# New landing places for the last raw weight pieces, and first products ahead of second sums in a chunked RWKV7 kernel

## The chip, the cores and the metric

The kernel runs on one core of a Trainium2 chip. The metric is the device time of one execution in microseconds (us), of which medians are quoted. Before the change it was 901.05 us (median of 3 runs, 900.12 to 902.5). All times inside an execution come from a profile of one execution and count from its first instruction. In the profile PE is TensorE, PEld its weight loads, DVE VectorE, ACT ScalarE, POOL GpSimd, and SPq the queue from which SyncE issues transfers. In the lines shown, `ph` is a PSUM bank of a first product, `gts` its Silu, `po` a bank of a sum (or of a merge), `wo_s` the converted w_out, `room` a landing place, `XI` and `mi` the inverse and its tile; `[2.06 <-DVE XI L426]` says that the engine was idle for 2.06 us until VectorE had written `XI` in line 426.

## The reference

```python
# r,k,v,w,a,b: (4 batches, 8 heads, 768 steps, 40 channels), float32
for t in range(S):
    y[:, :, t] = einsum('bhd,bhde->bhe', rt, state)
    Sa = einsum('bhde,bhe->bhd', state, at)
    state = state * wt[..., None] - einsum('bhd,bhe->bhde', Sa, bt) \
          + einsum('bhd,bhe->bhde', vt, kt)
x = y.transpose(0, 2, 1, 3).reshape(3072, 320)
h = x @ w_in                                  # 320 x 2048
return (h * (1 / (1 + exp(-h)))) @ w_out      # 2048 x 320
```

The weights `w_in` and `w_out` arrive as 64-bit floats and are turned into 32-bit floats on the chip.

## The kernel before

The recurrence is worked in 12 chunks of 64 steps. Each chunk pair needs the inverse of small triangular blocks: VectorE computes it row by row, stores it (`xd`), reads it back in another layout (`XT`), transposes it, and TensorE merges the blocks. After a merge come keys, right side, solve, readings, and the state products (`pgy`). When two chunks are done, their 256 or 512 columns of x go through the token stage: "first products" x @ w_in with a Silu by ScalarE, and "second sums" with w_out. All of TensorE's work runs in one order that a scheduler fixes at build time.

The raw weights come in 40 pieces. Each lands in a place, and is converted by five VectorE and three ScalarE operations.

```python
if n < NW // 2:           place = ("wi0", "wi1", "wo0", "wo1", "room")[n % 5]
elif n < NW * 3 // 4:     place = ("wo0", "wo1", "room")[(n - NW // 2) % 3]
else:                     place = ("mi", "tmp", "room")[(n - NW // 2) % 3]   # mi, tmp: the inverse's tiles
...
def weights(n, ...):                        # conversion: first part of piece n, second part of piece n - 1
    vector.tensor_scalar(e <- hi); vector.tensor_scalar(f <- hi)
    scalar.activation(e); scalar.activation(f); scalar.activation(lo)
    ...
    vector.scalar_tensor_tensor(e); vector.tensor_tensor(f <- f + lo); vector.tensor_tensor(weight <- f * e)
    load_weights(n)                         # the place is free: send for the next piece
...
def row(t):                                 # one row of the inverse
    vector.tensor_tensor(tmp <- X * M);  vector.tensor_reduce(X <- tmp)
def back():                                 # after the last row
    scalar.copy(mi[0:16] <- X);  vector.tensor_copy(mi[16:32] <- X);  send(sync, xd, mi)
...
ph = [moe_bank("ph") for _ in range(2)]     # first product: two of three banks, free again after its Silus
...
now = {2: 4, 3: 5}[n]                       # items of the token stage done beside chunks 2 and 3
```

## Time and profile before

| | before |
|---|---|
| median time | 901.05 us |
| span of the profiled execution | 899.2 us |
| TensorE / VectorE / ScalarE / GpSimd busy | 87% / 62% / 33% / 17% |
| mean granted TensorE clock | 0.946 (its record begins at 94.7 us) |

Busy shares say little here: TensorE looks full on average, but between 205 and 270 us it waits, runs at half clock (0.50 granted from 215 to 220 us) and waits again. The prediction shows the slices, stretches and orders of time from which this is read.

### The profile page before, as it was taken

The numbers are of one execution on the slowest core, as the hardware profiler recorded it, in microseconds if no ns is written. First come the engines' busy times: TensorE is split into PE (matmuls) and PEld (weight loads), VectorE is DVE, ScalarE is ACT, GpSimd is POOL, SyncE is SP. The second block draws the span as 40 slices with busy tenths as digits, with TensorE's granted clock in tenths as the row PEclk, the third lists the DMA queues.
The fourth block names the chain that finished last, engine by engine and source line by source line (L and its number), as shares of the span: only waits on it lengthen the run. The fifth ranks groups of instructions, "written<-read, shape, count | busy, mean of one in ns | idle before, by whom it ended". The sixth has DMA issues, their size and how long they took to land.

```text
span 899.2 us, 25358 instructions
## 1 busy us (share of the span) xinstructions
PE 778.9 (87%) x10914; PEld 552.9 (61%) x10914; DVE 557.9 (62%) x1084; ACT 297.4 (33%) x689; POOL 151.4 (17%) x156
## 2 busy tenths in 40 slices
PE   2145689896898997999998999999999989999995
PEld 2135677674786853875746857648757468574643
DVE  9979889885439598176896295982768912510000
ACT  2234358532622322514025342226140243311120
POOL 7312024200202201303102240113031000000001
PEclk9999869996759998999999999999999999999998
DMA  7875646744325542444613627325424021102001
GB/s 154 167 147 142 150 130 150 166 106 107 90 59 128 105 110 47 115 108 87 145 34 62 157 64 158 93 48 117 96 56 122 16 61 40 42 23 57 1 1 33
DMA packets 240151, 82.99 MB, mean 92 GB/s; under 512 B 207136, under 2 KB 231968, under 8 KB 240032
## 3 DMA queue, kind: packets, MB, share of 16 engines
q1 hardware_dynamic: 219488, 69.96, 34.8%
q10 hardware_dynamic: 20544, 11.34, 4.7%
q8 instruction: 87, 1.43, 0.7%
q14 instruction: 32, 0.26, 0.1%
HBM read 67.11 MB, written 14.16 MB: 90 GB/s over the span
## 4 chain that ended last, share of the span: by engine, by line
PE 45%; DVE 19%; DMA 3%; SPq 2%; issue 1%; ACT 1%; POOL 0%; POOLq 0%; ACTq 0%; DVEq 0%
PE po L825 14%; PE ph L813 9%; DVE tmp L419 7%; DVE XI L426 7%; PE pgy L264 4%; PE pl L264 3%; PE ph L818 3%; PE pm L264 2%; SPq L217 2%; PE pt L264 2%; PE pr L264 2%; PE po L264 2%; PE pq L264 2%; PE pu L264 2%; DVE GV L761 1%
## 5 line engine op out<-in xcount | busy, mean ns | idle before, releaser
L825 PE MATMUL po<-wo_s,gts 128*128 128x320 f32 x768 | 224.8, 448 | 17.1 <-ACT gts L820 10.8
L825 PEld LDWEIGHTS po<-wo_s,gts 128*128 128x128 f32 x768 | 145.2, 194 | 82.7 <-ACT gts L820 14.7
L813 PE MATMUL ph<-xt,wi_s 128*128 128x512 f32 (+1 forms) x448 | 182.2, 549 | 2.2 <-ACT ot L834 1.4
L813 PEld LDWEIGHTS ph<-xt,wi_s 128*128 128x128 f32 x448 | 82.1, 192 | 82.3 <-issue 67.9
L820 ACT ACTIVATE gts<-ph 128x512 f32<-128x512 f32 (+1 forms) x112 | 54.6, 531 | 161.1 <-PE ph L818 160.4
L722 DVE TENSOR_TENSOR vl<-pl,ml 128x512 f32<-128x512 f32 x48 | 30.9, 685 | 113.0 <-PE pl L264 77.6
L419 DVE TENSOR_TENSOR tmp<-XI,mi 64x2 f32<-64x2 f32 (+40 forms) x169 | 85.5, 506 | 8.8 <-DMA mi<-md 3.9
L841 POOL TENSOR_TENSOR ot<-gts,ot 128x320 f32<-128x320 f32 x24 | 21.8, 907 | 358.1 <-ACT gts L839 352.9
L336 DVE RECIPROCAL w<-W 128x512 f32<-128x512 f32 x24 | 80.3, 3347 | 1.3
L426 DVE TENSOR_REDUCE XI<-tmp 64x2 f32<-64x2 f32 (+40 forms) x169 | 77.0, 455 | 5.2
L264 PE MATMUL pq<-XT,sb 32*32 32x32 f32 (+1 forms) x1280 | 34.9, 207 | 32.6 <-DVE XT L463 21.1
L818 PE MATMUL ph<-xt,wl_s 64*128 64x512 f32 (+1 forms) x224 | 56.9, 585 | 0.0
L264 PE MATMUL pm<-a,kb 64*64 64x64 f32 x1280 | 41.5, 244 | 16.9 <-POOL kb L366 15.5
L264 PEld LDWEIGHTS pq<-XT,sb 32*32 32x32 f32 (+1 forms) x1280 | 31.6, 131 | 38.7 <-issue 16.0
L363 POOL TENSOR_TENSOR a<-a,W 64x512 f32<-64x512 f32 x32 | 39.5, 1236 | 75.4 <-DMA a<-in_aT 52.2
L1084 DVE TENSOR_SCALAR bad<-pb 1x1 int32<-1x1 f32 x1 | 0.1, 147 | 83.4 <-PE pb L1083 83.4
L264 PEld LDWEIGHTS pm<-a,kb 64*64 64x64 f32 x1280 | 38.1, 156 | 21.2 <-POOL kb L366 15.7
L839 ACT COPY gts<-po 128x320 f32<-128x320 f32 x24 | 10.2, 425 | 121.8 <-PE po L825 98.0
L264 PEld LDWEIGHTS pl<-r,vut 64*128 64x128 f32 x768 | 45.4, 189 | 4.7 <-ACT vl L650 2.1
L264 PE MATMUL pl<-r,vut 64*128 64x64 f32 x768 | 46.5, 274 | 2.0 <-ACT vl L650 2.0
L264 PE MATMUL pt<-ident,kb 128*128 128x128 f32 x192 | 29.1, 313 | 21.2 <-DVE a L308 21.2
L348 POOL TENSOR_TENSOR kb<-kb,w 128x512 f32<-128x512 f32 x20 | 24.8, 1238 | 131.9 <-DVE w L336 118.6
(108 smaller groups left out, 1060.7 us busy)
## 6 DMA issues: line engine op xcount, KB each, us to landing
kb<-in_bT SPq DMA_DIRECT2D x48, 128.0 KB
vut<-in_vT SPq DMA_DIRECT2D x48, 128.0 KB
r<-in_rT SPq DMA_DIRECT2D x24, 256.0 KB
w<-in_wT SPq DMA_DIRECT2D x45, 128.0 KB
kb<-in_kT SPq DMA_DIRECT2D x44, 128.0 KB
a<-in_aT SPq DMA_DIRECT2D x32, 128.0 KB
vl<-in_v SPq DMA_DIRECT2D x48, 80.0 KB
xs<-yx ACTq DMA_DIRECT2D x48, 80.0 KB
```

The lines of the kernel that those rows point to most:

```text
L264: x = what(*x, **y)
L336: pin(nc.vector.reciprocal(R, u.W[:, :, 1 : C + 1]))
L348: nc.gpsimd.tensor_tensor(out=u.kb[:, :, 1], in0=u.kb[:, :, 1], in1=R, op=ALU.mult)
L363: nc.gpsimd.tensor_tensor(out=u.a[J, j], in0=u.a[J, j], in1=u.W[J, :, 0:C], op=ALU.mult)
L419: x = nc.vector.tensor_tensor(out=part, in0=X[L, :, t + 1 : N, t + 1 : N], in1=M[L, :, t, t + 1 : N].unsqueeze(2).to_broadcast([hi - lo, I ...
L426: x = nc.vector.tensor_reduce(out=X[L, :, t + 1 : N, t], in_=part, axis=AX.X, op=ALU.add)
L722: nc.vector.tensor_tensor(out=u.vl[:, :, j, D:], in0=pl[j].rearrange("p (q t) -> p q t", q=Q), in1=ml.unsqueeze(1).to_broadcast([128, Q, C ...
L813: in_order(nc.tensor.matmul(ph[n], lhsT=wi_s[:, k, at : at + 128], rhs=xt[:, k, :], start=k == 0, stop=False))
L818: in_order(nc.tensor.matmul(ph[n], lhsT=wl_s[R, i, :], rhs=xt[R, 2, :], start=False, stop=True))
L820: nc.scalar.activation(out=place(2 * i + n)[:, T], in_=ph[n], func=AF.Silu)
L825: in_order(nc.tensor.matmul(po[:, 0:DM], lhsT=place(f)[:, b * 128 : b * 128 + 128], rhs=wo_s[:, NF // 2 * half + f, :], start=f == 0, stop ...
L841: nc.gpsimd.tensor_tensor(out=ot4, in0=rest, in1=ot4, op=ALU.add)
```

## The change

The intent: the last pieces land where nothing of the inverse waits for them (the k and b tiles of later chunks, and a stretch of w_out), and TensorE has eight first products to do before the first sum that needs the last weights.

```diff
-            elif n < NW * 3 // 4:
+            elif n < NW // 2 + 9:
                 place = ("wo0", "wo1", "room")[(n - NW // 2) % 3]
+            elif n == NW // 2 + 12:
+                place = "wo1"
             else:
-                place = ("mi", "tmp", "room")[(n - NW // 2) % 3]
+                place = ("room", "kb2", "kb3")[(n - NW // 2 - (8 if n < NW // 2 + 12 else 9)) % 3]
...
-            u.kb = sb.tile([128, Q, 2, C], F32, name="kb", bufs=6)
+            u.kb = sb.tile([128, Q, 2, C], F32, name="kb", tag=f"kb{(NM * u.n + u.m) % 6}")
...
         for half in range(2):
+            sums = []
             for c in range(2 if apart else 1):
                 steps += [partial(first, T, NF // 4 * half + i) for i in range(NF // 4)]
-                steps += [partial(second, half, b) for b in range(T.start // 128, T.stop // 128)]
+                sums += [partial(second, half, b) for b in range(T.start // 128, T.stop // 128)]
+                if half == 0 or c > 0 or not apart:
+                    steps += sums
+                    sums = []
...
-        for u in units[n + 2]:
+        for u in units[n + 2] if n == 3 else []:
             load(u)
-        now = {2: 4, 3: 5}[n]
+        now = {2: 6, 3: 4}[n]
-            weave(steps[0:4], queue[0:1], [x[i] for i in (0, 5, 1, 6)], convert[31:34])
+            weave(steps[0:4], queue[0:1], convert[31:])
...
-            convert[34:] if n == 2 else [],
```

After the change, a line of the kernel has a number 4 higher than before from the conversions on: the second sum is L829 and not L825, the Silu L824, the first product L817.

More of the change, by code (lines that the diff above doesn't have):

```diff
@@ L980 @@
         steps = [x for pair in zip(*[chain(u, xs) for u in units[n]]) for x in pair]
-        now = {2: 4, 3: 5}[n]
+        now = {2: 6, 3: 4}[n]
         x = prepare(n + 2)
         if n == 2:
-            weave(steps[0:4], queue[0:1], [x[i] for i in (0, 5, 1, 6)], convert[31:34])
-            scores = [x[i] for i in (2, 4, 7, 9, 3, 8)]
+            weave(steps[0:4], queue[0:1], convert[31:])
+            scores = [partial(load, u) for u in units[n + 2]] + [x[i] for i in (0, 5, 1, 6, 2, 4, 7, 9, 3, 8)]
         else:
```

## The prediction

> **What bounds the kernel now.** I read four views in this order. First the page's slices, for where TensorE has room: a slice is 899.2 / 40 = 22.5 us.
>
> ```profile
> PE   2145689896898997999998999999999989999995
> ...
> PEclk9999869996759998999999999999999999999998
> ```
>
> From slice 13 on (about 290 us) TensorE is busy at 9 or 10 tenths, except near 350 us, so late work is bounded by TensorE. Before that stand slices 9 to 11 (202 to 270 us): 6, 8 and 9 tenths, at a granted clock of 0.6, 0.7 and 0.5. That is where w_out's second half is converted from raw 64-bit words and where the inverse of chunks 2 and 3 is merged. Second, busy time in stretches there (TensorE, its weight loads, VectorE, ScalarE, GpSimd, then granted clock, DMA share, GB/s):
>
> ```profile
> 200.00:205.00 5.00, 5.00 (x24) 3.09 (x23) 4.90 (x14) 2.22 (x7) 0.00 (x0) 1.00 0.12 43
> 205.00:210.00 5.00, 2.89 (x14) 1.65 (x12) 2.19 (x7) 3.03 (x8) 0.00 (x0) 1.00 0.68 221
> 210.00:215.00 5.00, 1.41 (x2) 0.50 (x2) 1.54 (x6) 1.41 (x5) 0.00 (x0) 0.58 0.81 169
> 215.00:220.00 5.00, 3.25 (x106) 2.17 (x109) 4.21 (x8) 0.00 (x0) 0.00 (x0) 0.50 0.38 81
> ...
> 245.00:250.00 5.00, 2.83 (x38) 1.57 (x40) 2.58 (x7) 0.19 (x1) 0.80 (x2) 0.50 0.62 135
> ```
>
> At 205 us TensorE falls from full to a quarter busy and VectorE with it: both wait. Third, TensorE in order of time (start, length, line, operation, count, idle time before and its releaser); fourth, the same of VectorE and of SyncE, which issues the loads:
>
> ```profile
> 210.78 1.41 PE L825 MATMUL po<-wo_s,gts 128*128 128x320 f32 x2 [2.03 <-ACT gts L820]
> 215.88 1.44 PE L825 MATMUL po<-wo_s,gts 128*128 128x320 f32 x2 [3.68 <-DVE wo_s L190]
> ...
> 247.17 2.50 PE L825 MATMUL po<-wo_s,gts 128*128 128x320 f32 x4 [2.58 <-DVE wo_s L190]
> ```
>
> ```profile
> 208.60 0.29 DVE L178 TENSOR_SCALAR room<-room 128x256 int32<-128x256 int32 x1 [2.41 <-DMA room<-in_w_out]
> 213.73 0.30 DVE L178 TENSOR_SCALAR room<-room 128x256 int32<-128x256 int32 x1 [3.05 <-DMA room<-in_w_out]
> 215.74 3.63 DVE L463 STREAM_TRANSPOSE XT<-XT 32x512 f32<-32x512 f32 x5
> ...
> 235.38 0.29 DVE L178 TENSOR_SCALAR room<-room 128x256 int32<-128x256 int32 x1 [3.27 <-DMA room<-in_w_out]
> ```
>
> ```profile
> 215.88 18.08 SPq L217 DMA_DIRECT2D room<-in_w_out  x3
> ```
>
> The second sums (L825) stand in TensorE's order before the merges and wait for w_out; w_out waits for a conversion, that for its raw piece, and that for a place: three pieces take 18 us to be issued, because their places are the inverse's own tiles and the merge's scratch. While TensorE idles its clock halves, and the merges run slowly.
>
> [...]after 2.03 + 3.68 us of gaps the granted clock is 0.50, and two matmuls of L825 take 1.44 us where sixteen take 4.57 us later (0.57 for two). [...]a conversion that waits for its data holds what is behind it, as the 3.05 us before the transposes show. [...]xd to transposes is 206.68 to 215.74 us, write, reads and issue together.
>
> **The change part by part.**
>
> *Places.* In the new order of VectorE all 40 pieces are converted before the inverse's last row; before, 33 were by then, counting the one right after it, 35 at the first transpose, and the last at 270 us. Ahead of the first row stand 35 conversions and not 31; among the rows 5 and not 2. Removed: 3.68 + 2.58 us of waits for w_out, and in the second merge the 4 us (243.1 to 247.15) in which its scratch operation stood behind three conversions. Added: 7 to 8 conversions ahead of the transposes. One is five VectorE operations starting some 0.2 to 0.34 us apart (208.60 to 210.68 us with a wait of 0.37), so 1.5 us: 8 x 1.5 = 12 us. VectorE's idle time from 110 to 205 us is 10.4 us by the stretches (1.3, 2.8, 0.6, 2.0, 1.7, 2.0), much of it waits for raw pieces that three free places shorten. If all is filled the transposes come 1.6 us later, if half 7. I take 4: they start at 220 and not at 215.7.
>
> *Order of products.* A first product of 256 columns is 8 + 4 matmuls, 1.99 + 0.63 = 2.62 us. In the new order four more of them (10.5 us) follow the four that end at 208.75 us, so TensorE has work until 219.3 us in place of 2.03 + 3.68 us of waits. But the first of the merge's products was put behind the seventh of eight: TensorE stops at 197.2 + 7 x 2.62 = 215.5 us until a transpose is there, at about 220.7. [...]The eighth and two quarters of a sum then run cold, and the bulk of the merge's first products, at 218.7 before, starts at some 227.
>
> *What is won after it.* From there to the state products (pgy, 268.85 us before) is 50.2 us now. Warm, with sums of which none waits, I count 39.5 us: first merge 10.5 (its 32-row products take 1.26 us at full clock in later chunks, 3.2 to 3.4 here), kt, right side and solve 8.2, second merge 12 (now 19.2), masks and readings 6.9 (now 8.4), plus slack. So pgy starts at about 227 + 39.5 = 266.5: won 2.3 us. From pgy to the merge of chunks 4 and 5 (357 us) VectorE's chain binds, scores to loads to 39 us of rows, and should only move along.
>
> *One item more.* Ten items of the token stage instead of nine are done in chunks 2 and 3, so one of 4.5 us leaves the TensorE-bound part. The room for it is there: at 350 to 355 us TensorE idles 3.68 + 2.04 us. Against it: the sums that covered the load of the next x (issued 322.65, products from 326.76 us) are gone, 10 us of idle at a low clock; in each later pair 17.1 us of cover becomes 12.6, which ends about when x lands (issue ends 448.2 us, first product 454.26). I take 1.3 us for these. Sum: 2.3 + 4.5 - 1.3 = 5.5 us.
>
> *Side effect.* With a tag for each k and b tile the scheduler puts ten loads of chunks 2 and 3, 128 KB each, into the first 27 us, three ahead of the first score stores. DMA is free there (82, 52 and 65 GB/s at 15 to 30 us), but the first row waited just 0.30 us for its tile, so up to 1.5 us may be lost; later load queues get shorter. Net zero.
>
> Predicted: 901.05 - 5.5, near 895.5 us.
>
> **The rivals.** *The clock is saved whole.* If VectorE fills its idle time and the transposes come at 217 us, [...]the clock stays up, the merge's bulk starts at 221 and pgy at 260.5: 8 + 3 = 11 us, or 890. For it: the scheduler put the merge's products just there, so its model has the tile ready. Against: its model before likewise showed no 3.05 us load waits. *The conversions become the bound.* The second load of the inverse's tile stands behind four loads of pieces on SyncE's queue, two of which wait for conversions; and the xd store stands behind k, b, w and a of chunks 4 and 5, which wait for the last pieces. If this costs 9 us the transposes come at 225, pgy at 272, and the item moved ahead only pays for it: 901 to 902. For it: VectorE is busy 39.4 of 40 us at 130 to 170. *The later order eats it.* If the exposed x loads cost 2 us in each of the four pairs, 899. Against: they fall where TensorE awaits the merge anyway.
>
> **Range and chances.** The transposes' arrival moves the result from 890 to 902, most likely 893 to 898; the start adds 1.5 us either way. Eight times in ten 887 to 902. Faster by over 2% means under 883 us: it needs all 13 us of idle time at 205 to 255 us and the cold part, and no delay: 0.05. Slower by over 2%, over 919 us, needs a stall of which the order shows no sign: 0.02. Within 2%: 0.93.
>
> **What would show it.** In TensorE's order of time no L825 waits for wo_s any more; its next gap is the merge's pq behind the seventh or eighth first product, waiting for the transpose of XT. In VectorE's, no conversion after the transposes, and the first transpose at 217 to 224 us. In the stretches, 205 to 220 us near full, a dip of the clock near 220, and none at 245 to 265. The state products of chunk 2 start some 2 us earlier, and the first 512-column product follows a gap. Rows beginning after 197 us, a transpose after 225 us or first scores stored later than 23 us would make the prediction too low; a clock that never falls there would make it too high.

## More of the kernel before

One more view of before is needed later, ScalarE in order of time (start, length, line, operation, count, idle time before it and what ended that):

```profile
205.58 1.07 ACT L435 COPY mi<-XI 128x512 f32<-128x512 f32 x1 [2.06 <-DVE XI L426]
206.56 0.65 ACT L820 ACTIVATE gts<-ph 128x256 f32<-128x256 f32 x2
```

ScalarE idles 2.06 us for the inverse's last row, copies, and only then does two Silus (L820).

## The result, and the profile after

The changed kernel took 909.17 us (median of 4 runs, 906.98 to 910.25) against 900.75 us of before on the same chip. The ratio is 1.0087, with a 95% interval from 1.0063 to 1.0111. A ratio is the mean time of one kernel's fast runs over that of the other's in the same rounds, so it isn't quite the ratio of the medians. A later repetition gave 1.0040. "Within 2%" held, but the time left the range, on the slow side.

The slices of the page of the changed kernel (905.1 us, so 22.6 us each):

```profile
PE   2135689998889659999998999999999989999996
...
PEclk9655868998769789999999999999999999999999
```

Counted from 0, slices 9 to 12 read 8, 8, 8, 9, so no slice there is full, and a new dip, 6 and 5, stands in slices 13 and 14 (294 to 339 us); it holds the 7.82 us for which TensorE waits for the next x, up to 339.55 us. The clock row misleads: in slices 1 to 3 it fell from 9, 9, 9 to 6, 5, 5, from 20 to 90 us by the stretches from 1.00 to 0.59. That makes up the fall of the mean from 0.946 to 0.914 (0.41 x 70 us = 29 us, and 0.032 x 905 us = 29 us). But the trace of before has no record of the clock ahead of 94.7 us, where that of the changed kernel begins at 25.2 us, and a time without a record counts as full clock: before reads 1.00 from 20 to 90 us. The products were as slow in both. Before, changed, and the same product later in the changed kernel, warm:

```profile
79.42 3.27 PE L264 MATMUL pq<-XT,sb 32*32 32x32 f32 x61 [8.17 <-DVE XT L514]
...
79.95 3.27 PE L268 MATMUL pq<-XT,sb 32*32 32x32 f32 x61 [8.32 <-DVE XT L518]
...
370.62 1.17 PE L268 MATMUL pq<-XT,sb 32*32 32x32 f32 x62 [0.38 <-DVE XT L467]
```

So the fall of the mean is no effect of the change; in the other executions of before the mean lies between 0.899 and 0.949. The sums at 188.5 us start within 0.1 us of before.

Busy time in stretches of the changed kernel (columns as in the prediction):

```profile
205.00:210.00 5.00, 4.68 (x22) 3.12 (x23) 4.90 (x10) 1.20 (x4) 2.79 (x2) 1.00 0.67 167
210.00:215.00 5.00, 1.86 (x7) 1.25 (x6) 2.91 (x5) 1.61 (x3) 0.00 (x0) 0.79 0.55 162
215.00:220.00 5.00, 5.00 (x15) 3.11 (x13) 1.62 (x3) 0.66 (x2) 0.00 (x0) 0.52 0.57 122
```

The stall moved from 205-210 to 210-215 us. It is followed by 5 us of full work at half clock. TensorE in order of time names the wait:

```profile
205.32 1.13 PE L817 MATMUL ph<-xt,wi_s 128*128 128x256 f32 x4 [1.28 <-ACT gts L824]
...
213.85 2.08 PE L817 MATMUL ph<-xt,wi_s 128*128 128x256 f32 x4 [3.14 <-ACT gts L824]
...
217.01 3.34 PE L817 MATMUL ph<-xt,wi_s 128*128 128x256 f32 x8
...
227.32 1.34 PE L829 MATMUL po<-wo_s,gts 128*128 128x320 f32 x4
...
239.76 2.50 PE L829 MATMUL po<-wo_s,gts 128*128 128x320 f32 x4
```

No sum waits for w_out any more. But a first product waits 3.14 us for a Silu (`gts`, L824), and the eight matmuls at 217.01 us take 3.34 us where eight warm ones take 1.99. Why is the Silu late? ScalarE:

```profile
212.45 1.07 ACT L439 COPY mi<-XI 128x512 f32<-128x512 f32 x1 [4.67 <-DVE XI L430]
213.42 0.65 ACT L824 ACTIVATE gts<-ph 128x256 f32<-128x256 f32 x2
```

It is the pair of lines that was shown of before, 6.9 us later. The products of these Silus were done at 209.6 us, but in ScalarE's order the inverse's copy is ahead of them and waits for the last row. And the last row is late; VectorE and then GpSimd in order of time:

```profile
196.45 0.42 DVE L194 TENSOR_TENSOR wo_s<-room 128x256 f32<-128x256 f32 x1
...
196.88 0.28 DVE L182 TENSOR_SCALAR room<-room 128x256 int32<-128x256 int32 x1
...
201.21 1.21 DVE L194 TENSOR_TENSOR wo_s<-room 128x256 f32<-128x256 f32 x1
...
202.93 1.14 DVE L182 TENSOR_SCALAR room<-room 128x256 int32<-128x256 int32 x1
...
206.53 1.41 DVE L194 TENSOR_TENSOR wo_s<-room 128x256 f32<-128x256 f32 x1
...
208.34 1.01 DVE L423 TENSOR_TENSOR tmp<-XI,mi 128x338 f32<-128x338 f32 x1
...
218.31 3.63 DVE L467 STREAM_TRANSPOSE XT<-XT 32x512 f32<-32x512 f32 x5 [5.27 <-DMA XT<-xd]
```

```profile
200.71 1.43 POOL L352 TENSOR_TENSOR kb<-kb,w 128x512 f32<-128x512 f32 x1 [52.85 <-ACT room L185]
202.74 1.18 POOL L344 TENSOR_TENSOR kb<-kb,w 128x512 f32<-128x512 f32 x1 [0.60 <-DMA kb<-in_kT]
206.19 1.47 POOL L352 TENSOR_TENSOR kb<-kb,w 128x512 f32<-128x512 f32 x1 [2.27 <-DMA kb<-in_kT]
207.62 1.36 POOL L344 TENSOR_TENSOR kb<-kb,w 128x512 f32<-128x512 f32 x1
```

Two things stand among the rows: conversions (L182, L194 and others), and operations that take two to four times as long as elsewhere (the first two lines; L423 of this size took 0.51 us before) while GpSimd multiplies k and b of chunk 4. Each of the four long ones ends within 0.4 us of the end of a GpSimd operation. In the kernel before GpSimd does nothing from 190 to 206 us.

Where the 5.9 us between the two profiled executions (905.1 - 899.2) come from, by milestones:

| milestone | before | after | difference |
|---|---|---|---|
| first of the half's first products | 197.2 | 197.3 | +0.1 |
| the last row has ended, copy starts | 205.6 | 212.4 | +6.9 |
| first transpose | 215.7 | 218.3 | +2.6 |
| bulk of the first merge's products | 218.7 | 228.6 | +9.9 |
| state products of chunk 2 | 268.9 | 279.0 | +10.1 |
| state products of chunk 3 | 306.8 | 321.1 | +14.4 |
| keys of chunk 4 | 358.9 | 371.7 | +12.9 |
| last state products | 799.3 | 812.2 | +12.9 |
| end of the last sum | 888.8 | 898.0 | +9.2 |
| end | 899.2 | 905.1 | +5.9 |

The medians differ by 8.4 us, and in the repetition by 5.2; single executions differ by a few us.

### The profile page after: what moved, and what is told of

Read it like the earlier page. It is cut to its first block, busy times and chain, and to the rows that moved or that the text cites.

```text
span 905.1 us, 25356 instructions
## 1 busy us (share of the span) xinstructions
PE 781.6 (86%) x10914; PEld 550.2 (61%) x10914; DVE 557.5 (62%) x1084; ACT 296.4 (33%) x689; POOL 150.6 (17%) x156
## 4 chain that ended last, share of the span: by engine, by line
PE 55%; DVE 33%; DMA 4%; issue 3%; ACT 3%; SPq 1%; POOL 1%; ACTq 0%; POOLq 0%; DVEq 0%
PE po L829 15%; PE ph L817 11%; DVE tmp L423 8%; DVE XI L430 8%; PE pgy L268 5%; PE pl L268 4%; PE ph L822 3%; PE po L268 3%; PE pt L268 3%; PE pq L268 3%; PE pu L268 2%; DVE w L340 2%; PE pr L268 2%; PE pm L268 2%; DVE GV L765 1%
## 5 line engine op out<-in xcount | busy, mean ns | idle before, releaser
L829 PE MATMUL po<-wo_s,gts 128*128 128x320 f32 x768 | 227.7, 452 | 10.7 <-ACT gts L824 9.3
L817 PE MATMUL ph<-xt,wi_s 128*128 128x512 f32 (+1 forms) x448 | 186.5, 559 | 15.0 <-DMA xt<-xs 8.7
L829 PEld LDWEIGHTS po<-wo_s,gts 128*128 128x128 f32 x768 | 146.8, 196 | 76.7 <-ACT gts L824 11.9
L817 PEld LDWEIGHTS ph<-xt,wi_s 128*128 128x128 f32 x448 | 83.6, 197 | 97.3 <-issue 69.4
L824 ACT ACTIVATE gts<-ph 128x512 f32<-128x512 f32 (+1 forms) x112 | 54.5, 532 | 196.4 <-PE ph L822 194.8
L423 DVE TENSOR_TENSOR tmp<-XI,mi 64x2 f32<-64x2 f32 (+40 forms) x169 | 84.5, 500 | 9.8 <-DMA mi<-md 5.1
L430 DVE TENSOR_REDUCE XI<-tmp 64x2 f32<-64x2 f32 (+40 forms) x169 | 76.7, 454 | 4.8
L845 POOL TENSOR_TENSOR ot<-gts,ot 128x320 f32<-128x320 f32 x24 | 20.9, 872 | 325.7 <-ACT gts L843 322.2
L268 PE MATMUL pm<-a,kb 64*64 64x64 f32 x1280 | 39.2, 235 | 17.5 <-POOL kb L370 15.5
L268 PE MATMUL pq<-XT,sb 32*32 32x32 f32 (+1 forms) x1280 | 30.1, 202 | 25.7 <-DVE XT L467 14.5
L843 ACT COPY gts<-po 128x320 f32<-128x320 f32 x24 | 10.2, 425 | 125.9 <-PE po L829 114.0
L268 PEld LDWEIGHTS pm<-a,kb 64*64 64x64 f32 x1280 | 36.0, 148 | 22.7 <-POOL kb L370 15.7
L268 PEld LDWEIGHTS pq<-XT,sb 32*32 32x32 f32 (+1 forms) x1280 | 27.3, 124 | 32.4 <-issue 16.0
L268 PE MATMUL pt<-ident,kb 128*128 128x128 f32 x192 | 26.9, 298 | 22.8 <-DVE a L312 22.8
L312 DVE TENSOR_TENSOR a<-pm,ml 64x512 f32<-64x512 f32 x48 | 33.0, 687 | 18.8 <-PE pm L268 18.0
```

Source lines behind the costliest of these rows:

```text
L268: x = what(*x, **y)
L312: x = nc.vector.tensor_tensor(out=u.a[O, j], in0=pm[O].rearrange("p (q t) -> p q t", q=Q), in1=ml[O].unsqueeze(1).to_broadcast([C, Q, C]), ...
L423: x = nc.vector.tensor_tensor(out=part, in0=X[L, :, t + 1 : N, t + 1 : N], in1=M[L, :, t, t + 1 : N].unsqueeze(2).to_broadcast([hi - lo, I ...
L430: x = nc.vector.tensor_reduce(out=X[L, :, t + 1 : N, t], in_=part, axis=AX.X, op=ALU.add)
L817: in_order(nc.tensor.matmul(ph[n], lhsT=wi_s[:, k, at : at + 128], rhs=xt[:, k, :], start=k == 0, stop=False))
L824: nc.scalar.activation(out=place(2 * i + n)[:, T], in_=ph[n], func=AF.Silu)
```

## The experiments

The start of the half's first products differs by up to 3.6 us between executions (196.7 to 200.3 us), whatever the kernel, so milestones of the experiments count from it. The theory after the comparison had two parts: conversions among the rows delay the inverse and, through ScalarE's queue, the Silus; and quarter sums stand between the merge's steps. Rivals: the order of products itself, the earlier loads, the throttle alone. All runs were correct; one run of before, in the third group, was slow and is left out. The first four kernels shared a chip and its runs of the kernel before; so did the next four, the next three and the last two. The wait for "gts" is the longest that TensorE spends on a Silu of the half's first products.

**order_only**: before, with the loop of the second half and `now` of the change, nothing else.

```diff
-                steps += [partial(second, half, b) ...]
+                sums += [partial(second, half, b) ...]     # as in the change
-        now = {2: 4, 3: 5}[n]
+        now = {2: 6, 3: 4}[n]
```

> The kernel before with the order of the products alone (eight first products ahead of the four sums, ten items of the token stage in place of nine); places, tags and loads stay as before. Theory (the loss of 8.4 us has two parts: conversions among the inverse's rows hold ScalarE's copy and with it the Silus, about 8 us by the start of the merge; quarter sums between the merge's products, about 2 us more than they cost before; and the item moved ahead gives 4.5 us back): here only two conversions stand among the rows, so they end near 206 us, no gap of 3 us waits for gts, the merge's first products run near 219 us, but the sums still stand between the merge's steps: 896 to 903 us. Rival (the order itself is the loss, whatever the places): 905 to 910 us.

Measured: 903.26 us against 903.27, ratio 0.9986 (0.996 to 1.0012). The rows ended 8.6 us after the first product (before 8.4), the longest wait for gts in this stage was 0.86 us. The rival falls: the order by itself costs nothing, and gains nothing either. State products of chunk 2 came 77.1 us after the first product (before 71.6), which the item moved ahead would about pay back.

**places_only**: the changed kernel with the old order of products.

```diff
-        now = {2: 6, 3: 4}[n]
+        now = {2: 4, 3: 5}[n]          # and steps += [second ...] directly after each four firsts
```

> The changed kernel with the old order of the products (four firsts, two sums, four firsts, two sums; nine items); places, tags and loads as changed. Theory: the conversions among the rows stay, so the rows end near 212 us and ScalarE's copy still stands ahead of Silus, but TensorE has sums to do there that need no Silu of a late product: the gap for gts is shorter, yet the transposes come at 218 us and not 215.7, so pgy of chunk 2 starts 2 to 6 us later than 268.85, and no item is moved ahead: 902 to 909 us. Rival (only the order costs): at or below the time before, 895 to 901 us.

Measured: 915.06 us, ratio 1.0132 (1.0103 to 1.016). That is worse than expected: the rows ended 15.7 us after the first product. The loss belongs to the places.

**act_free**: the changed kernel, ScalarE's half of the copy given to VectorE.

```diff
-            nc.scalar.copy(out=mi[L, 0:16], in_=turned[L, 0:16])
+            if N == 16 and hi - lo == 128:
+                nc.vector.tensor_copy(out=mi[L, 0:16], in_=turned[L, 0:16])
+            else:
+                nc.scalar.copy(out=mi[L, 0:16], in_=turned[L, 0:16])
```

> The changed kernel, with ScalarE's half of the inverse's last copy (chunks 2 and 3 only) given to VectorE. Theory (Silus queued behind that copy on ScalarE stop TensorE for 3.14 us, and the clock falls after it): the gap before the first product at 213.85 us shrinks below 1 us, the clock stays at 0.9 or more from 205 to 220 us, the first products end near 221 us in place of 227.3, and the kernel is 4 to 7 us faster than the changed one: 902 to 905 us. The copy costs VectorE 0.6 us ahead of the transposes. Rival (the first products run late for another cause, such as the throttle alone): the gap goes, the clock falls nevertheless, 907 to 910 us.

Measured: 906.55 us, ratio 1.0033 (0.9994 to 1.0072). The stretches of this run:

```profile
210.00:215.00 5.00, 5.00 (x26) 3.45 (x24) 3.81 (x7) 1.32 (x4) 0.00 (x0) 1.00 0.55 155
215.00:220.00 5.00, 2.54 (x14) 1.88 (x14) 1.26 (x2) 0.66 (x2) 0.00 (x0) 0.94 0.59 150
```

The gap is gone and the clock stays up, so the copy in ScalarE's queue was the cause of the stall. The first products ended at 225.6 us, not near the 221 that was expected. The state products of chunk 2 came 76.2 us after the first product, not 81.7. In time the interval overlaps that of the unaltered kernel, so what this stall costs at the end isn't separated from zero. TensorE now stops later, for the transpose.

**sums_late**: the changed kernel, the four sums of the second half behind the merge of chunk 3.

```diff
+                    mark["merged"] = product(...).ins          # in the merge's last product
...
+                if n0 == 0 and half == 1 and f == 0:
+                    behind(x, mark["merged"])                   # order on TensorE only
```

> The changed kernel with the four second sums of chunks 0 and 1 (second half) held behind the last product of the merge of chunk 3; nothing else moved by hand. Theory (the quarter sums between the merge's steps stand on the path): the time from the merge's first products to pgy of chunk 2 falls from 50.3 us to 40 to 44 us, the sums go into the idle time before the 512-column products (7.82 us wait for xt and the rows' chain), and the kernel is 4 to 9 us faster than the changed one: 900 to 905 us. Rival (the sums fill time in which the merge waits for VectorE and ScalarE anyway, and keep the clock up): the merges take as long without them, the clock there is lower, and the time stays 907 to 912 us.

Measured: 899.84 us, ratio 0.9973 (0.9947 to 0.9999): faster than the changed kernel. But from the merge's bulk to the state products it took 46.9 us, not 40 to 44; 3.1 us more were won between the state products of chunks 2 and 3 (39.0 in place of 42.2). TensorE in the first merge of this run:

```profile
228.84 0.25 PE L268 MATMUL po<-XT,qq 32*16 32x16 f32 x8 [0.62 <-DVE qq L488]
...
230.74 0.22 PE L268 MATMUL po<-XT,qq 32*16 32x16 f32 x3 [1.19 <-issue]
...
234.47 0.23 PE L268 MATMUL po<-qq,XT 32*32 32x16 f32 x1 [1.82 <-issue]
...
235.58 3.27 PE L268 MATMUL pq<-XT,sb 32*32 32x32 f32 x61 [0.51 <-DVE XT L518]
```

Even without a sum, one step, the completion of the corners, lasts from 228.84 to about 235 us, and the clock falls (0.6 in the page's slices from 224 to 269 us): the 61 products after it take 3.27 us, where 62 of this form take 1.17 to 1.19 us when warm.

**conv_late**: the changed kernel, conversions of the last three pieces behind the last row.

```diff
+            after_rows = lambda x: behind(x, mark["row"])
+            convert[37:] = [partial(weights, i, after_rows) for i in range(37, NW + 1)]
             weave(steps[0:4], queue[0:1], convert[31:])
```

> The changed kernel with the conversions of the last three pieces (37, 38, 39) held behind the inverse's last row, so that they run while the inverse's tile is stored and read back; the sums stay between the merge's steps. Theory (the changed places lose because conversions stand among the rows: the rows ended at 212.4 us and not 205.6, the Silus waited behind ScalarE's copy): rows end near 208 us, transposes at 213 to 215 us, no gap of 3 us for gts, and the kernel is 4 to 8 us faster than the changed one: ratio to before 0.999 to 1.005. Rival (the places lose by their tags and the earlier loads, or the sums are all of it): rows end earlier but the time stays within 2 us of the changed kernel, ratio 1.007 to 1.010.

Measured: 897.28 us against 904.11, ratio 0.9922 (0.9898 to 0.9946), more than was expected. The stretches and VectorE's order:

```profile
205.00:210.00 5.00, 5.00 (x24) 3.21 (x23) 4.79 (x11) 1.80 (x5) 0.00 (x0) 1.00 0.00 0
210.00:215.00 5.00, 4.15 (x21) 2.72 (x20) 4.11 (x14) 3.77 (x12) 0.00 (x0) 1.00 0.65 194
215.00:220.00 5.00, 5.00 (x28) 3.36 (x24) 4.37 (x8) 1.32 (x4) 0.00 (x0) 1.00 0.75 127
```

```profile
208.97 0.60 DVE L440 COPY mi<-XI 128x512 f32<-128x512 f32 x1
...
216.00 3.63 DVE L467 STREAM_TRANSPOSE XT<-XT 32x512 f32<-32x512 f32 x5
```

The conversions fill the 7 us in which the inverse is stored and read back, when VectorE idled 5.27 us in the changed kernel. Rows ended 8.9 us after the first product, the longest wait for gts was 1.13 us, the clock never fell from 205 to 220 us, and state products of chunk 2 came after 72.1 us. More than the conversions moved here: GpSimd's products of chunk 4 and the loads for them came after the rows too (pool_late, below), and what each of them is worth in time isn't separated.

**conv_sums**: both repairs.

> Both repairs: the last three conversions behind the rows, and the four second sums behind the merge of chunk 3. Theory (two separate losses that add: sums_late won 11 us against the changed kernel's ratio, act_free 5 us by the same stall that this one removes): 4 to 8 us below sums_late: ratio to before 0.989 to 0.993. Rival (the two repairs win the same idle time): the ratio of sums_late, 0.996 to 0.999.

Measured: 894.68 us, ratio 0.9894 (0.987 to 0.9919): the version that beats both kernels, 1.1% under before. The further gain over conv_late is 2.6 us by the medians, less than the sums were worth alone; the intervals just overlap.

**order_sums**: order_only with the sums behind the merge, as in sums_late.

> The kernel before with the order of the products (as in order_only) and the sums behind the merge of chunk 3; places, tags and loads as before. Theory (the new places are worth nothing by themselves, the order wins once the sums are out of the merge): order_only stood at 0.9986, so 4 to 9 us less: ratio 0.989 to 0.995. Rival (without the new places the sums or the merge's scratch wait for conversions: the scratch operation of the second merge stood behind three conversions up to 247 us): ratio 0.997 or above.

Measured: 901.39 us, ratio 0.9963 (0.9933 to 0.9992). It fell between theory and rival. The new places are therefore worth something once the conversions are off the rows (conv_sums, with the same sums: 0.9894).

**tags_only**: before, with a tag of its own for each k and b tile.

```diff
-            u.kb = sb.tile(..., name="kb", bufs=6)
+            u.kb = sb.tile(..., name="kb", tag=f"kb{(NM * u.n + u.m) % 6}")
```

> The kernel before with a tag of its own for each k and b tile, nothing else: ten loads of chunks 2 and 3 go out in the first 27 us. Theory (the hoisted loads cost nothing, as the traces agree up to 197 us): ratio 0.998 to 1.002. Rival (part of the loss of the changed places, 11.8 us in places_only, is from the hoisted loads or from what the tags do later): 1.004 or above.

Measured: 901.9 us against 904.11, ratio 0.9983 (0.9951 to 1.0015). The rival falls: the tags cost nothing.

**after_again**: the changed kernel unaltered, beside the two that follow.

> The changed kernel unaltered, beside the repaired ones on the same chip. Ratio to before 1.006 to 1.011 as on the first chip (1.0087); if the chip or the day mattered, the ratio would fall outside.

Measured: 906.12 us against 900.88, ratio 1.0040 (1.0002 to 1.0078), below the expected span. Its rows ended 15.1 us after the first product and the wait for gts was 3.14 us, both as the first time. The size of the loss is known to be between 0 and 1% and no better; its sign and its place are.

**conv_one**: as conv_late, for the last piece alone (`convert[39:]`).

> A dose: only the conversion of the last piece (39) is held behind the inverse's last row, not of the last three. Theory (each conversion among the rows delays the rows by some 1.5 us, and the stall for gts goes as the copy moves ahead): rows end about 13 us after the first of the half's first products started (8.9 with three held, 15.1 with none), the gap for gts is 1 to 2.5 us, ratio to before 1.001 to 1.006, between the changed kernel (1.0087) and three held (0.9922). Rival (what helps is something else than the number of conversions, such as the order of SyncE's queue): ratio equal to one of the two ends.

Measured: 908.87 us, ratio 1.0068 (1.0027 to 1.0109). Rows ended after 12.1 us, as expected, but the gap for gts was 1.97 us and the clock still fell, to 0.60 from 212 to 215 us. Less than the whole repair gave no gain in time: the rows moved as the theory had it, but the ratio lies with the unaltered kernel's, as the rival had it. In this run two of GpSimd's products were among the rows, in conv_late none.

**conv_pgy**: as conv_sums, but the sums wait for the state products of chunk 2.

```diff
+                mark["written", (be + j) % 2] = product(...).ins   # in the state products
...
+                    behind(x, mark["written", 0]); behind(x, mark["written", 1])
```

> As conv_sums, but the four sums wait for the last state product of chunk 2 and not for the merge of chunk 3, so that no sum stands between the state products of its second pair. Theory (the sum in the middle of the state products delays VectorE's chain to the next state): pgy of chunk 3 follows that of chunk 2 within 38 us (39.9 in conv_sums), ratio to before 0.986 to 0.989. Rival (the products of masks there, not the sum, set the time): ratio as conv_sums, 0.989 to 0.991.

Measured: 895.02 us, ratio 0.9922 (0.9885 to 0.9958), no better than conv_sums. State products of chunk 3 followed after 42.4 us and not 39.9. TensorE there:

```profile
295.73 1.13 PE L268 MATMUL pm<-stage,kb 64*64 64x64 f32 x32 [8.82 <-POOL kb L352]
...
299.47 1.13 PE L268 MATMUL pm<-stage,kb 64*64 64x64 f32 x32 [2.61 <-POOL kb L352]
```

The theory falls. Without sums there TensorE just waits 8.82 us for GpSimd, and the products that follow run cold (1.13 us where 0.69 is warm).

**pool_late**: the changed kernel, GpSimd's four products of chunk 4 behind the last row. conv_late had moved both conversions and these products; this run moves the products alone.

```diff
             x = nc.gpsimd.tensor_tensor(out=u.kb[:, :, 1], in0=u.kb[:, :, 1], in1=R, op=ALU.mult)
+            if u.n == 4:
+                behind(x, mark["row"], Sync)        # likewise for kb[:, :, 0]
```

> The changed kernel, with the four GpSimd products of k and b with the reciprocals of chunk 4 held behind the inverse's last row; conversions and sums as changed. In the changed kernel these four run at 200 to 209 us, among the rows, and four VectorE operations beside them took 1.21, 1.14, 1.41 and 1.01 us where their like take 0.42, 0.29, 0.42 and 0.51: 3.1 us together; in the kernel before, and with the last three conversions held, no GpSimd work falls there. Theory (of the 6.7 us by which the rows end later, some 3 are this contention, and the rest the three more conversions): no VectorE operation among the rows takes over 0.7 us, the rows end some 12 us after the half's first product (15.1 in the changed kernel, 8.9 with three conversions held), the gap for gts shrinks from 3.14 to 1 to 2 us, ratio to before 1.000 to 1.007. Rival (the lengthened operations are idle time that would pass anyway, all 6.7 us are the conversions): rows end 15 us after, ratio 1.004 to 1.010.

Measured: 904.47 us against 904.22, ratio 0.9997 (0.9955 to 1.0039). The rows ended 11.9 us after the first product, no operation among them took over 0.7 us, and the wait for gts was 1.42 us, with the clock at 1.00 from 205 to 215 us. So 3.2 of the 6.7 us of the rows' delay were contention between VectorE and GpSimd (the four lengthened operations had lost 3.1 us), and the other 3.5, by difference, the conversions. In time the interval overlaps that of the unaltered kernel. The transposes did not come earlier (20.9 us after the first product, 21.0 in the changed kernel). SyncE's queue shows what took up most of the gain:

```profile
209.67 0.34 SPq L221 DMA_DIRECT2D xd<-mi  x1
212.52 1.89 SPq L221 DMA_DIRECT2D w<-in_wT  x3
214.50 4.29 SPq L221 DMA_DIRECT2D XT<-xd  x8
```

From the store of the inverse to its reading back it was 2.64 us in the changed kernel (213.54 to 216.18 us), here 4.83: three loads of w stand ahead, and the queue waited 2.4 us for one of the moved products (`kb`, L344). The moved products held up SyncE's queue.

**pool_sums**: pool_late and sums_late together.

> As pool_late, with the four sums behind the merge of chunk 3 as well. Theory (the repairs add): 2 to 4 us below sums_late (0.9973), ratio 0.992 to 0.996, and above conv_sums (0.9894), in which the conversions left the rows too. Rival: as sums_late, 0.996 to 0.999.

Measured: 895.36 us, ratio 0.9926 (0.9884 to 0.9968). That is what repairs that add would give, but the interval overlaps that of sums_late (0.9947 to 0.9999), so that they add isn't shown.

| kernel | last row after first product, us | longest wait for gts in the half's first products, us | state products of chunk 2 after first product, us | ratio to before |
|---|---|---|---|---|
| before | 8.4 | 0.86, then 2.03 before a sum | 71.6 | 1 |
| changed | 15.1 | 3.14 | 81.7 | 1.0087, 1.0040 |
| pool_late | 11.9 | 1.42 | 80.9 | 0.9997 |
| conv_one | 12.1 | 1.97 | 83.8 | 1.0068 |
| conv_late | 8.9 | 1.13 | 72.1 | 0.9922 |
| conv_sums | 9.4 | 1.66 | 70.4 | 0.9894 |

## Why the prediction was right or wrong

**The start: right.** "Net zero" for the hoisted loads; tags_only confirms it.

**The transposes: right in time, by a wrong route.** Predicted at 220 us, measured 218.31. The prediction counted conversions and got their sum right, but it didn't ask where the rows end. They ended 6.9 us later, and 3.2 of those were contention with GpSimd, which the prediction didn't mention: the loads of k and b of chunk 4, which before stood behind raw pieces on SyncE's queue until 234.07 us, were issued from 196.94 us on, and GpSimd's products of them started among the rows. The way from the last row to the transposes shrank from 10.2 to 5.9 us. The reading back of xd was issued 3.7 us after the copy began and not 5.3 (before, the load of a raw piece at 210.51 us stood ahead of it), and the transposes followed 2.1 us later and not 4.9 (before, a conversion that waited 3.05 us for its piece stood ahead of them).

The trace shows it in single operations. Beside GpSimd's products the two-input operations L194 and L423 took 1.21, 1.41 and 1.01 us, where their like take 0.42, 0.42 and 0.51, and the one-input L182 took 1.14 us in place of 0.29; each ends 0.15 to 0.37 us after a GpSimd product does. Not every operation beside them was lengthened: the reductions (L430) that started at 201.01 and 207.87 us took 0.28 and 0.44 us, against 0.28 and 0.45 for the same sizes before. With the products moved (pool_late), none among the rows took over 0.7 us. What decides which operation is held up isn't shown.

**"TensorE has work until 219.3 us in place of 2.03 + 3.68 us of waits": this step failed.** It counted the products and not their banks. A first product needs two of three banks, and a bank comes free by a Silu. The Silus stand in ScalarE's queue behind a copy that waits for the last row. The prediction had seen an operation hold up those behind it on VectorE (the 3.05 us before the transposes), and didn't ask the same of ScalarE, where the copy waited 4.67 us with two Silus behind it. Measured: 3.14 us of stall, clock at 0.52 after it, first products done at 227.3 and not 219.3 us. act_free shows that the copy made the stall, pool_late and conv_late that the late rows made the copy late. So the merge's bulk began 9.9 us later than before, not 8.3 (227 - 218.7) as predicted: near by luck, since the predicted loss stood for another wait, that for the transpose.

**"Warm, with sums of which none waits, I count 39.5 us": this step failed, and it is the largest error.** Measured 50.4 us, as before (50.2). The waits of sums for w_out did go, but the sums still stood in the merge's way at half clock (four matmuls took 2.50 us where 1.34 is warm). Taking them out gave 3.5 us of it (sums_late, 46.9). Part of the rest is a term that the sum left out: the merges of chunks 2 and 3 have the corner step that the later chunks, from which 10.5 us was taken, lack. The first merge took 14.5 us in sums_late, and the two "issue" gaps shown there are 3.0 us of it. No run came below 46.9 us. What makes these gaps no run tested, but the kept traces point to a cause: in the 15 profiled executions all 67 gaps of TensorE of that name over 0.6 us (after 100 us) end 1.2 to 1.6 us after a packet of 16 KB of the DMA queue q8 has ended (the four of before and the five of the changed kernel 1.28 to 1.52 us after), of which there are 87 in each execution; by chance some 4 in 100 would. The profile's page lists this queue's kind as "instruction". That TensorE waits there for its own instructions is a guess, not shown.

**"From pgy ... should only move along": off by 2.7 us.** From state products of chunk 2 to keys of chunk 4 it took 92.7 us and not 90.0.

**The clock.** The prediction put the half clock of before down to "2.03 + 3.68 us of gaps" together. Its own lines say more: the two matmuls at 210.78 us, after the first gap alone, took 1.41 us, as slow as those after the second (1.44), and the granted clock was 0.70 from 210 to 212 us and 0.50 from 212 to 220 us.

**"One item more": right, and a little under.** From the last state products to the end of the last sum 3.7 us were won (4.5 predicted). The 1.3 us that were set against it for the later order did not show: the distance to before is 12.9 us at the keys of chunk 4 and at the last state products. After the last sum another 3.3 us were won, which nothing predicted: 10.4 us to the end became 7.1. The final check's product, which stood behind the last sum, is done at 825 us now. Yet order_only has it early too and takes 9.3 us, and places_only has it late and takes 8.0, so the cause stays open.

Summed in the prediction's way, with measured terms: -10.1 - 2.7 + 3.7 + 3.3 = -5.8 us, where the prediction had +2.3 + 4.5 - 1.3 = +5.5. The measured difference of the profiled executions is -5.9.

**The rivals.** "The conversions become the bound" came nearest: it named the direction and 901 to 902 us. It expected queued loads to delay the store, which did not happen. Its core, conversions ahead of the inverse's end, is what conv_late and pool_late show: about 3.5 us of the rows' delay. With three conversions moved a few us the same change gives 0.9922, 7 us less than before, beyond the gain that was predicted. Of the other two rivals, the clock wasn't saved, and the later order cost little in the later pairs: TensorE waited 8.7 us for x in all, 7.82 of them before 339.55 us.

## What to carry to other kernels

When a change frees a buffer, ask which queued work it releases, on every engine, and what that work will then stand in front of. Follow a freed stall through each engine's order of work, ScalarE's evictions included (here a copy that waited 4.67 us stood ahead of two Silus, and a product waited 3.14 us for them): "TensorE has work" means that it has work and a free bank. Work that nobody waits for yet belongs into the round trip of a transfer (here conversions filled 7 us in which VectorE had idled for 5.27). And before a mean clock is compared, look whether both traces have a record of it for the whole time: products of one form, side by side, tell.

## What was measured of the hardware

- The granted clock fell after single gaps of TensorE of 3.14 us (changed kernel: 1.00 from 205 to 210 us, 0.52 from 215 to 220 us), of 2.03 us (before: 1.00 from 205 to 210 us, 0.70 from 210 to 212 us, 0.50 from 212 to 220 us) and of 1.97 us (conv_one: 1.00 in the 3 us that held the gap, 0.60 in the next 3 us). After one of 1.66 us (conv_sums) the next eight matmuls of a first product still took 1.99 us, as when warm. These are single cases, in which the work ahead of the gaps differs too.
- Four operations of VectorE's chain lost 0.79, 0.85, 0.99 and 0.50 us beside GpSimd operations of 1.2 to 1.5 us; taking those away moved the chain's end by 3.2 us (15.1 to 11.9 us after the first product).
- The gaps named "issue" took 1.19 and 1.82 us in the corner step of sums_late and 2.06 us in that of the changed kernel. Their cause wasn't tested.
